# Contiguous first loads, and scaling by a diagonal product, in the first eight passes of a block-causal attention and expert-layer kernel

## The chip, the core and the metric

The kernel runs on one core of a Trainium2 chip. A core has five engines with instruction queues of their own: TensorE (PE in the profile; its weight loads are PEld), VectorE (DVE), ScalarE (ACT), GpSimd (POOL) and SyncE (SP), which here issues the transfers. Each queue is worked in order; engines wait for one another through semaphores. Matrix products read SBUF and write PSUM. The metric is the device time of one execution in microseconds, lower is better.

## The reference

Attention over 8 batches and 8 heads, sequence 576, head size 64, with a mask in blocks of 64: a query block sees the key blocks up to its own. Its output, with the heads side by side, goes through a layer that expands 512 to 2048, applies the square of the ReLU, and contracts again.

```python
scores = scale * np.matmul(q, k.transpose(0, 1, 3, 2))
mask = block_i >= block_j
scores = np.where(mask, scores, -1000000000.0)
scores = scores - np.max(scores, axis=-1, keepdims=True)
attn = np.exp(scores)
attn = attn / (np.sum(attn, axis=-1, keepdims=True) + 1e-09)
return np.matmul(attn, v).astype(np.float32)
...
h = x @ w_in
r = np.maximum(h, 0.0)
g = r * r
return (g @ w_out).astype(np.float32)
```

The expert layer's weights come in as 64-bit floats; the kernel makes a high and a low 16-bit part of each.

## The kernel before

**Passes.** Heads are worked in pairs: a pass holds one batch and one pair, with the two heads in the two halves of the 128 partitions. Of the first two batches, the eight passes 0 to 7 (`G_X`, the short passes) take only the query blocks 0, 1 and 2, that is 64, 128 and 192 keys. This gives the first 192 tokens of both batches, 384 in all, which make the first chunk of the expert layer. The query blocks 3 to 8 of these batches follow in passes 8 to 15 and later batches in whole passes; all those run interleaved with products of the expert layer.

**A short pass.** `softmax` does the scores of the three query blocks into one PSUM tile (L450, fp32 products, keys of 64 partitions by head, with the query padded by zeros in the other half), their negated maxima (L488 and L503, DVE), the exponentials with their sums into the tile `p32` (L506, ACT), the sums' reciprocals `rs` (L514 on POOL, L515 on DVE), and then copies each query block's row out of `p32`, scaled by its reciprocal, into `x_rows`: the block of 192 keys on ACT (L521, `XR_ACT` = 1), the two others on DVE (L523). `x_rows` has five slots (`SLOTS`). `turn` transposes its four 128 x 128 blocks on PE against the identity (L560), and copies the result to `x_turned` (L562, ACT in these passes). `values` multiplies by the values (L593) and copies the output to `x` (L600, ACT). Columns that no key fills were set to zero once (L136, L137).

**First loads.** `load_first` brings two passes at a time (four calls), in five transfers: the queries of each head half (L346, two, 96 KB each), the keys (L347, 192 KB), and the values of each of the two passes (L350, 128 KB each). The tile holds, per partition, pass by pass the padded queries of head 0, those of head 1, and the keys. POOL zeroes the padding (L345). The contiguous runs are 768 bytes for queries and keys and 512 for values. Between the calls SP issues expert weights (`load_w1`, L268): `AHEAD` = (0, 1, 1, 1) blocks after the four calls, and the rest of the 16 behind them. Of each block POOL takes low bits (L231) and DVE a maximum (L281); `BS` lists for the first seven blocks the pass behind whose last scaled row (`t["mark"]`) DVE may do so. From the maxima come power-of-two scales per group of four blocks (`pow2_of_max`, L187 to L196, and L290), and from these the 16-bit parts (`weight_parts`, L322 to L327).

**Then.** When the four pairs of a batch are done, `normalize` forms the power-of-two scale of each token from the squares (L639, L651, L656, L668 to L670). With both batches normalized and the first weight parts there, `first_moe` runs (products L734 and L759). `spin` puts filler products on PE at a few places (L213).

**Order.** The program order is not the order of the queues: a scheduler with a simulated timeline (`TLS`) sets each engine's order when the kernel is built. `behind` adds an edge of order without a wait.

The buffers of the short passes (`p_rows`, `p_turned`) are used again by the later passes' rows, `y_rows` and `p_blocks`; `clear_y` and `clear` set their empty columns to zero on POOL.

Of the kernel before, what the change touches and what calls it, by code (L numbers as in the profile page):

```python
# [8 lines left out]
F32 = mybir.dt.float32  # L9
# [5 lines left out]
AF = mybir.ActivationFunctionType  # L15
ALU = mybir.AluOpType
# [3 lines left out]
P = 128  # L20
D = 64
# [45 lines left out]
XR_ACT = 1  # L67
# [6 lines left out]
T3 = 192  # L74
# [8 lines left out]
SLOTS = 5  # L83
# [17 lines left out]
def attention_moe_kernel(ctx: ExitStack, tc: tile.TileContext, qkt, qk, vm, vt, w_in, w_out, out):  # L101
    nc = tc.nc
# [25 lines left out]
    rows32 = p_rows.bitcast(F32)  # L128
# [3 lines left out]
    x_rows = rows32.rearrange("p (s j k) -> p s j k", s=SLOTS, k=2 * P)  # L132
# [3 lines left out]
    nc.vector.memset(x_rows[:, :, 0, D:P], 0.0)  # L136
    nc.vector.memset(x_rows[:, :, 2, 3 * D :], 0.0)  # L137
# [194 lines left out]
    def load_first(b, hp):  # L332

        n = NHP // 2 * b + hp // 2
        if n < 2:
            t = p2.tile([P, 2, 3, T3], F32, tag="kT", name=f"first{n}")
        elif n == 2:
            t = p1.tile([P, 2, 3, T3], F32, tag="xt1", name=f"first{n}")
        else:
            t = p2.tile([P, 2, 3, T3], F32, tag="qk32", name=f"first{n}", bufs=3)  # L340
        v = vraw[n] if n < 2 else p2.tile([P, 2, 5, D], F32, tag="v16", name=f"firstv{n}")
        hps = slice(hp, hp + 2)
        for h in range(2):
            hs, zs = slice(D * h, D * h + D), slice(D - D * h, P - D * h)
            nc.gpsimd.memset(t[zs, :, h], 0.0)  # L345
            nc.sync.dma_start(t[hs, :, h], qkt[b, hps, hs, 0, :T3].rearrange("c p s -> p c s"))  # L346
        nc.sync.dma_start(t[:, :, 2], qkt[b, hps, :, 1, :T3].rearrange("c p s -> p c s"))  # L347
        for c in range(2):
            o = v[:, c, 0:4].rearrange("p (h n) d -> p h n d", h=2)
            nc.sync.dma_start(o, vm[b, hp + c, :, :, 0:2, :])  # L350
            passes[NHP * b + hp + c].update(
                qz=[t[:, c, h] for h in range(2)], kf=t[:, c, 2], chunks=2, v32=o, es=D**-0.5
            )
# [116 lines left out]
    def softmax(t, group, complete):  # L470
# [6 lines left out]
        p32 = p2.tile([P, 1024], F32, tag="p32", name=f"p32_{gu}")  # L477
# [26 lines left out]
        for i, (j, off) in enumerate(group):  # L504
            w = D * (j + 1)
            nc.scalar.activation(  # L506
                p32[:, off : off + w],
                ps[:, off : off + w],
                AF.Exp,
                bias=nmx[:, i : i + 1],  # L510
                scale=es if t["native"] else -1.0,
                accum_out=sm[:, i : i + 1],
            )
        nc.gpsimd.tensor_scalar(sm, sm, 1e-9, 2.0**-A_P, op0=ALU.add, op1=ALU.mult)  # L514
        nc.vector.reciprocal(rs, sm)  # L515
        if t["whole"]:
            for i, (j, off) in enumerate(group):
                w = D * (j + 1)
                o = (y_rows[:, j - 3] if t["first"] else x_rows[:, t["i"] % SLOTS, j])[:, 0:w]
                if t["first"] or i < XR_ACT:  # L520
                    nc.scalar.activation(o, p32[:, off : off + w], AF.Copy, scale=rs[:, i : i + 1])  # L521
                else:
                    t["mark"] = nc.vector.tensor_scalar(  # L523
                        o, p32[:, off : off + w], rs[:, i : i + 1], None, op0=ALU.mult
                    )
            turn(t, group)
            return
# [12 lines left out]
    def turn(t, group):  # L540
# [11 lines left out]
        else:  # L552
            blocks = [x_rows[:, s, j, P * c : P * c + P] for j, c in ((0, 0), (1, 0), (2, 0), (2, 1))]
            todo = [(blocks, x_turned[:, s])]
        pool, tag = (ps_m, "mm") if t["i"] < PT_MM else (ps_x, "x")
        for blocks, o in todo:
            m = len(blocks)
            pt = pool.tile([P, 4, P], F32, tag=tag, name=f"pt_{n_turned}")
            for i, blk in enumerate(blocks):
                nc.tensor.transpose(pt[:, i], blk, ident)  # L560
# [391 lines left out]
```

## Time and profile before

| what | us |
|---|---|
| median of 3 runs | 1059.64 |
| lowest, highest | 1056.55, 1062.74 |
| the profiled execution | 1060.85 |
| its span, first to last instruction | 1058.6 |
| ACT busy in the span | 657.3 |
| DVE busy in the span | 711.6 |
| POOL busy in the span | 75.8 |

The page's slices of the whole span, each 26.5 us, show where the engines are full (tenths of busy time, 9 is 90% or more; PEclk is the granted clock of TensorE in tenths; DMA is the mean busy share of the 16 transfer engines):

```profile
PE   7899999999999999999999999999999999999998
...
DVE  5998787777787898688379579759677626132230
ACT  6697885794796699289278579449658515041230
...
PEclk8899999999999999999999999999999999999999
DMA  8786168686986788478456758557917520000000
```

The eight short passes lie in the first slice and the beginning of the second. Times of the trace are given from the start of the span. A bracket at the end of a timeline row is the idle time of that engine before the row's first instruction, and what ended it.

### The profile page before, as it was taken

The numbers are of one execution on the slowest core, as the hardware profiler recorded it, in microseconds if no ns is written. First come the engines' busy times: TensorE is split into PE (matmuls) and PEld (weight loads), VectorE is DVE, ScalarE is ACT, GpSimd is POOL, SyncE is SP. The second block draws the span as 40 slices with busy tenths as digits, with TensorE's granted clock in tenths as the row PEclk, the third lists the DMA queues.
The fourth block names the chain that finished last, engine by engine and source line by source line (L and its number), as shares of the span: only waits on it lengthen the run. The fifth ranks groups of instructions, "written<-read, shape, count | busy, mean of one in ns | idle before, by whom it ended". The sixth has DMA issues, their size and how long they took to land.

```text
span 1058.6 us, 19069 instructions
## 1 busy us (share of the span) xinstructions
PE 1014.5 (96%) x6899; PEld 542.6 (51%) x6899; DVE 711.6 (67%) x1972; ACT 657.3 (62%) x1668; POOL 75.8 (7%) x183
## 2 busy tenths in 40 slices
PE   7899999999999999999999999999999999999998
PEld 5445444454554554455455455455455555455553
DVE  5998787777787898688379579759677626132230
ACT  6697885794796699289278579449658515041230
POOL 4213130000000000000001001000000000000000
PEclk8899999999999999999999999999999999999999
DMA  8786168686986788478456758557917520000000
GB/s 271 268 286 240 49 203 201 112 163 141 177 170 140 150 155 158 96 142 184 94 119 123 160 118 166 118 113 140 170 32 121 96 58 1 20 11 11 20 1 30
DMA packets 303902, 133.11 MB, mean 126 GB/s; under 512 B 275648, under 2 KB 288960, under 8 KB 303808
## 3 DMA queue, kind: packets, MB, share of 16 engines
q1 hardware_dynamic: 303808, 131.90, 56.5%
q8 instruction: 54, 0.88, 0.3%
q14 instruction: 40, 0.33, 0.1%
HBM read 55.31 MB, written 9.44 MB: 61 GB/s over the span
## 4 chain that ended last, share of the span: by engine, by line
PE 38%; issue 28%; ACT 8%; DVE 8%; DMA 5%; POOL 2%; SPq 0%; POOLq 0%; ACTq 0%; DVEq 0%
PE po L759 21%; PE ph L734 14%; ACT p L506 2%; ACT p_rows L532 2%; PE ps L461 2%; DVE ps L492 2%; PE px L593 2%; DMA p_turned<-p_rows 2%; DMA kT<-k 1%; DMA qT<-qs 1%; POOL sm L514 1%; DVE p_rows L533 1%; ACT r L742 1%; ACT r L740 1%; DVE g L744 1%
## 5 line engine op out<-in xcount | busy, mean ns | idle before, releaser
L734 PE MATMUL ph<-xt,w1h 128*128 128x384 f16 x1536 | 378.0, 327 | 4.4 <-ACT r L740 4.2
L759 PE MATMUL po<-w2h,g 128*128 128x512 f16 x1152 | 352.4, 380 | 3.6 <-ACT r L740 2.0
L759 PEld LDWEIGHTS <-g 128*128 128x128 f16 x1728 | 165.9, 98 | 202.4 <-issue 11.5
L734 PE MATMUL ph<-xt,w1l 128*128 128x384 f16 x768 | 251.0, 327 | 0.0
L759 PE MATMUL po<-w2l,g 128*128 128x512 f16 x576 | 218.8, 380 | 0.7 <-DVE w2l L327 0.7
L506 ACT ACTIVATE p<-ps,nmx 128x192 f32<-128x192 f32 (+8 forms) x288 | 149.0, 532 | 109.7 <-DVE nmx L492 86.2
L734 PEld LDWEIGHTS <-w1h 128*128 128x128 f16 x1536 | 143.3, 98 | 110.0 <-issue 21.0
L740 ACT ACTIVATE r<-ph 128x384 f32<-128x384 f32 x192 | 94.1, 493 | 120.2 <-PE ph L734 119.1
L533 DVE SCALAR_TENSOR_TENSOR p_rows<-p,rs,p_rows 128x384 f16<-128x384 f32 (+4 forms) x264 | 128.9, 525 | 22.1 <-ACT p_rows L532 18.4
L532 ACT ACTIVATE p_rows<-p,rs 128x384 f16<-128x384 f32 (+4 forms) x264 | 125.3, 550 | 14.3 <-DVE rs L515 9.7
L492 DVE CUSTOM_DVE_ANT_0 ps<-ps,zero,es 128x128 f32<-128x128 f32 (+8 forms) x216 | 117.5, 550 | 23.8 <-PE ps L461 22.3
L766 DVE TENSOR_SCALAR ob<-po,uv 128x512 f32<-128x512 f32 x36 | 29.1, 808 | 142.7 <-PE po L759 142.7
L744 DVE TENSOR_TENSOR g<-r,g 128x384 f16<-128x384 f32 x192 | 105.5, 553 | 2.9
L743 DVE CAST g<-r 128x384 f16<-128x384 f32 x192 | 67.0, 353 | 59.0 <-ACT r L742 58.9
L742 ACT ACTIVATE r<-r 128x384 f32<-128x384 f32 x192 | 100.8, 530 | 2.7
L734 PEld LDWEIGHTS <-w1l 128*128 128x128 f16 x768 | 75.3, 98 | 49.4 <-issue 0.5
L514 POOL TENSOR_SCALAR sm<-sm 128x2 f32<-128x2 f32 (+2 forms) x104 | 37.6, 362 | 697.9 <-ACT p L506 591.8
L461 PE MATMUL ps<-kT,qT 128*64 128x64 f16 (+6 forms) x960 | 80.8, 290 | 6.9 <-ACT p L506 3.0
L593 PE MATMUL px<-p_turned,v 128*64 128x64 f16 (+5 forms) x1168 | 76.5, 270 | 7.1 <-DMA p_turned<-p_rows 5.6
L593 PEld LDWEIGHTS <-v 128*64 128x64 f16 x1128 | 53.5, 110 | 32.8 <-issue 21.6
L461 PEld LDWEIGHTS <-qT 128*64 128x64 f16 x960 | 45.2, 110 | 41.5 <-issue 27.7
L506 ACT ACTIVATION_READ_ACCUMULATOR p<-ps,nmx 128x1 f32 x288 | 60.6, 211 | 0.0
(139 smaller groups left out, 859.0 us busy)
## 6 DMA issues: line engine op xcount, KB each, us to landing
qk<-in_qk SPq DMA_DIRECT2D x24, 576.0 KB, 4.9
wa<-in_w_out SPq DMA_DIRECT2D x16, 512.0 KB, 5.7
out<-ob SPq DMA_DIRECT2D x32, 256.0 KB, 2.3
vraw<-in_vm SPq DMA_DIRECT2D x30, 256.0 KB, 3.7
w1raw<-in_w_in SPq DMA_DIRECT2D x8, 512.0 KB, 6.7
wb<-in_w_out SPq DMA_DIRECT2D x8, 512.0 KB, 5.1
kf<-in_qkt SPq DMA_DIRECT2D x8, 288.0 KB, 4.1
w2h<-in_w_in SPq DMA_DIRECT2D x4, 512.0 KB, 9.7
```

The costliest lines, as they stand in the source:

```text
L461: nc.tensor.matmul(ps[hs, o].rearrange("p (n d) -> p n d", d=D), t["qT"][:, j, hs], t["kT"][:, z, c0:c1, hs], start=(z == 0), stop=(z == 1),)
L492: nc.vector.tensor_tensor_reduce(ps[:, off : off + w], ps[:, off : off + w], zero.to_broadcast([P, w]), es, 3e38, op0=ALU.add, op1=ALU.min ...
L506: nc.scalar.activation(p32[:, off : off + w], ps[:, off : off + w], AF.Exp, bias=nmx[:, i : i + 1], scale=es if t["native"] else -1.0, acc ...
L532: nc.scalar.activation(hi, p, AF.Copy, scale=rs[:, i : i + 1])
L533: nc.vector.scalar_tensor_tensor(lo, p, rs[:, i : i + 1], hi, op0=ALU.mult, op1=ALU.subtract)
L593: nc.tensor.matmul(px[hs, D * a :].rearrange("p (j d) -> p j d", d=D), lhs, rhs, start=(c == 0 and pi == 0), stop=(c == NCH[g] - 1 and (pi ...
L734: nc.tensor.matmul(ph[:, :CH], w[:, f, P * cc : P * cc + P], xt[:, z, cc, :], start=(i == 0), stop=(i == 11))
L740: nc.scalar.activation(r, ph[:, :CH], AF.Relu, scale=c)
L742: nc.scalar.activation(r, r, AF.Square)
L743: nc.vector.tensor_copy(g[:, 0], r)
L744: nc.vector.tensor_tensor(g[:, 1], r, g[:, 0], op=ALU.subtract)
L759: nc.tensor.matmul(po, gs[f][:, z, P * t : P * t + P], w[:, f, :], start=(i == 0), stop=(i == 3 * NF - 1))
```

## The change

Three things change, all for the short passes.

1. The host lays out two more inputs, `qk1` and `v1`. A pair of passes is loaded by three transfers: for each head half, queries and keys together, in runs of 3072 bytes (keys and queries lie in the other order for the second half, so that the key rows of both halves meet in the middle third of the tile); and the values of both passes, in runs of 1024 bytes. The tile's layout is now queries of head 0, keys, queries of head 1, each for both passes.
2. The exponentials are written straight into the slot of `x_rows`, unscaled, instead of into `p32`. The copies that scaled them go. DVE instead makes three diagonal matrices, the identity times the reciprocals, in one operation, in the same slot (`x_diag`).
3. The four blocks of a pass are turned by fp32 products with those matrices as the moving operand, which turn and scale at once, instead of by transposes against the identity. There are four slots instead of five, of seven blocks each. The mark for the weight maxima is now the diagonal operation.

```diff
-SLOTS = 5
+SLOTS = 4
...
-    x_rows = rows32.rearrange("p (s j k) -> p s j k", s=SLOTS, k=2 * P)
+    x_slots = rows32[:, : SLOTS * 7 * P].rearrange("p (s b k) -> p s b k", s=SLOTS, k=P)
+    x_rows, x_diag = x_slots[:, :, 0:4], x_slots[:, :, 4:7]
...
-    nc.vector.memset(x_rows[:, :, 0, D:P], 0.0)
-    nc.vector.memset(x_rows[:, :, 2, 3 * D :], 0.0)
+    for b in (1, 3):
+        nc.vector.memset(x_rows[:, :, b, D:P], 0.0)
...
+        shape = [P, 3, 2, T3]
...
-            nc.gpsimd.memset(t[zs, :, h], 0.0)
-            nc.sync.dma_start(t[hs, :, h], qkt[b, hps, hs, 0, :T3].rearrange("c p s -> p c s"))
-        nc.sync.dma_start(t[:, :, 2], qkt[b, hps, :, 1, :T3].rearrange("c p s -> p c s"))
+            nc.gpsimd.memset(t[zs, 2 * h], 0.0)
+            nc.sync.dma_start(t[hs, h : h + 2], qk1[n, hs])
+        nc.sync.dma_start(v[:, :, 0:4], v1[n])
         for c in range(2):
-            o = v[:, c, 0:4].rearrange("p (h n) d -> p h n d", h=2)
-            nc.sync.dma_start(o, vm[b, hp + c, :, :, 0:2, :])
...
-        p32 = p2.tile([P, 1024], F32, tag="p32", name=f"p32_{gu}")
+        short = t["whole"] and not t["first"]
+        if short:
+            p32 = x_rows[:, t["i"] % SLOTS].rearrange("p b k -> p (b k)")
+            at = {2: 0, 1: 2 * P, 0: 3 * P}
...
+        if short:
+            t["mark"] = nc.vector.tensor_tensor(
+                x_diag[:, t["i"] % SLOTS],
+                ident[:, None, :].to_broadcast([P, n, P]),
+                rs[:, :, None].to_broadcast([P, n, P]),
+                op=ALU.mult,
+            )
+            turn(t, group)
+            return
...
-                if t["first"] or i < XR_ACT:
-                    nc.scalar.activation(o, p32[:, off : off + w], AF.Copy, scale=rs[:, i : i + 1])
-                else:
-                    t["mark"] = nc.vector.tensor_scalar(
-                        o, p32[:, off : off + w], rs[:, i : i + 1], None, op0=ALU.mult
-                    )
...
-            blocks = [x_rows[:, s, j, P * c : P * c + P] for j, c in ((0, 0), (1, 0), (2, 0), (2, 1))]
+            blocks = [(x_rows[:, s, b], x_diag[:, s, j]) for b, j in ((3, 2), (2, 1), (0, 0), (1, 0))]
...
-                nc.tensor.transpose(pt[:, i], blk, ident)
+                if t["first"]:
+                    nc.tensor.transpose(pt[:, i], blk, ident)
+                else:
+                    nc.tensor.matmul(pt[:, i], blk[0], blk[1], start=True, stop=True)
...
+    qk1 = qkt[..., :T3].reshape(2, 2, 2, P, 2, T3).transpose(0, 1, 3, 4, 2, 5).reshape(4, P, 2, 2, T3)
+    qk1 = np.concatenate([qk1[:, :D], qk1[:, D:, ::-1]], axis=1)
+    v1 = vm[:2, :, :, :, :2].reshape(2, 2, 2, P, 4, D).transpose(0, 1, 3, 2, 4, 5).reshape(4, P, 2, 4, D)
```

More of the change, by code (lines that the diff above doesn't have):

```diff
@@ L334, in load_first @@
         n = NHP // 2 * b + hp // 2
+        shape = [P, 3, 2, T3]
         if n < 2:
-            t = p2.tile([P, 2, 3, T3], F32, tag="kT", name=f"first{n}")
+            t = p2.tile(shape, F32, tag="kT", name=f"first{n}")
         elif n == 2:
-            t = p1.tile([P, 2, 3, T3], F32, tag="xt1", name=f"first{n}")
+            t = p1.tile(shape, F32, tag="xt1", name=f"first{n}")
         else:
-            t = p2.tile([P, 2, 3, T3], F32, tag="qk32", name=f"first{n}", bufs=3)
+            t = p2.tile(shape, F32, tag="qk32", name=f"first{n}", bufs=3)
         v = vraw[n] if n < 2 else p2.tile([P, 2, 5, D], F32, tag="v16", name=f"firstv{n}")
-        hps = slice(hp, hp + 2)
         for h in range(2):
             hs, zs = slice(D * h, D * h + D), slice(D - D * h, P - D * h)
-            nc.gpsimd.memset(t[zs, :, h], 0.0)
-            nc.sync.dma_start(t[hs, :, h], qkt[b, hps, hs, 0, :T3].rearrange("c p s -> p c s"))
-        nc.sync.dma_start(t[:, :, 2], qkt[b, hps, :, 1, :T3].rearrange("c p s -> p c s"))
+            nc.gpsimd.memset(t[zs, 2 * h], 0.0)
+            nc.sync.dma_start(t[hs, h : h + 2], qk1[n, hs])
+        nc.sync.dma_start(v[:, :, 0:4], v1[n])
         for c in range(2):
-            o = v[:, c, 0:4].rearrange("p (h n) d -> p h n d", h=2)
-            nc.sync.dma_start(o, vm[b, hp + c, :, :, 0:2, :])
             passes[NHP * b + hp + c].update(
-                qz=[t[:, c, h] for h in range(2)], kf=t[:, c, 2], chunks=2, v32=o, es=D**-0.5
+                qz=[t[:, 2 * h, c] for h in range(2)],
+                kf=t[:, 1, c],
+                chunks=2,
+                v32=v[:, c, 0:4].rearrange("p (h n) d -> p h n d", h=2),
+                es=D**-0.5,
             )
@@ L506, in softmax @@
             nc.scalar.activation(
-                p32[:, off : off + w],
+                p32[:, at[j] : at[j] + w],
                 ps[:, off : off + w],
@@ L518, in softmax @@
                 w = D * (j + 1)
-                o = (y_rows[:, j - 3] if t["first"] else x_rows[:, t["i"] % SLOTS, j])[:, 0:w]
-                if t["first"] or i < XR_ACT:
-                    nc.scalar.activation(o, p32[:, off : off + w], AF.Copy, scale=rs[:, i : i + 1])
-                else:
-                    t["mark"] = nc.vector.tensor_scalar(
-                        o, p32[:, off : off + w], rs[:, i : i + 1], None, op0=ALU.mult
-                    )
+                o = y_rows[:, j - 3, 0:w]
+                nc.scalar.activation(o, p32[:, off : off + w], AF.Copy, scale=rs[:, i : i + 1])
             turn(t, group)
@@ L943 @@
     arrays, args = {}, []
-    for name, a in (("qkt", qkt), ("qk", qk), ("vm", vm), ("vt", vt), ("w_in", w1), ("w_out", w2)):
+    for name, a in (("qk1", qk1), ("v1", v1), ("qkt", qkt), ("qk", qk), ("vm", vm), ("vt", vt), ("w_in", w1), ("w_out", w2)):
         arrays[f"in_{name}"] = a
```

7 lines of the change are left out of this document (5 added, 2 removed).

## The prediction, made before the changed kernel was run

> **What bounds the kernel now.** First the page, for the engine that sets the length.
>
> ```profile
> span 1058.6 us, 19069 instructions
> ...
> PE 1014.5 (96%) x6899; PEld 542.6 (51%) x6899; DVE 711.6 (67%) x1972; ACT 657.3 (62%) x1668; POOL 75.8 (7%) x183
> ```
>
> TensorE (PE) is busy for 96% of the span. Busy time by stretch (length, then PE, PEld, DVE, ACT, POOL with their instruction counts, clock, DMA share, GB/s) shows where the missing 44 us lie:
>
> ```profile
> core 0: us, PE busy (x) PEld busy (x) DVE busy (x) ACT busy (x) POOL busy (x), PEclk, DMA share, GB/s
> 0.00:50.00 50.00, 39.75 (x304) 26.03 (x305) 37.46 (x118) 31.78 (x98) 19.94 (x52) 0.86 0.84 275
> 50.00:100.00 50.00, 46.87 (x283) 25.53 (x280) 45.51 (x115) 42.72 (x99) 12.13 (x23) 0.97 0.83 282
> ```
>
> Ten of the 44 idle us are in the first 50, at a mean granted clock of 0.86. The change touches only the eight short passes there and what loads them, so I treat the kernel as a front that ends when the first product of the expert layer starts, and a rest that begins when the front ends. A microsecond saved in the front is worth at most one at the end. The timeline of the front shows what releases what:
>
> ```profile
> 5.28 1.67 PE L450 MATMUL ps<-first 128*64 128x192 f32 x24 [0.72 <-DMA first<-in_qkt]
> 8.86 0.97 PE L450 MATMUL ps<-first 128*64 128x192 f32 x12 [1.91 <-ACT p L506]
> 11.49 1.54 PE L560 MATMUL pt<-ident,p_rows 128*128 128x128 f32 x6
> 13.86 1.53 PE L450 MATMUL ps<-first 128*64 128x192 f32 x11 [0.83 <-DMA first<-in_qkt]
> 17.88 0.33 ACT L600 ACTIVATE x<-px 128x192 f32<-128x192 f32 x1 [1.16 <-PE px L593]
> 25.34 0.66 PE L593 MATMUL px<-p_turned,firstv 128*64 128x192 f32 x8 [1.16 <-ACT p_turned L562]
> 27.15 0.36 DVE L656 TENSOR_SCALAR hb<-nq 128x192 int32<-128x192 int32 x1 [0.53 <-PE nq L213]
> 47.54 0.33 PE L734 MATMUL ph<-xt,w1h 128*128 128x384 f16 x1
> ```
>
> Read as three stages. Up to 17.9 us, PE and the loads lead: PE waits for the first loads (5.28) and the third (13.86), and ScalarE (ACT) waits for PE (17.88). From there to about 27 ACT leads: PE waits for ACT's copy at 25.34. From 27.15 to 47.54 VectorE (DVE) leads. The stretches agree:
>
> ```profile
> 10.30:13.00 2.70, 2.70 (x19) 2.16 (x18) 1.68 (x10) 2.08 (x8) 0.50 (x1) 0.57 1.01 278
> 13.00:17.80 4.80, 3.97 (x33) 3.40 (x34) 2.50 (x11) 2.33 (x9) 2.02 (x6) 0.53 1.01 279
> 17.80:25.00 7.20, 6.01 (x68) 4.49 (x64) 5.36 (x20) 7.12 (x31) 3.07 (x9) 1.00 1.02 399
> 30.00:40.00 10.00, 6.18 (x50) 4.09 (x49) 10.00 (x25) 2.56 (x6) 6.15 (x10) 0.90 1.04 338
> ```
>
> PE runs at 0.57 and 0.53 of its clock from 10.3 to 17.8; ACT is busy 7.12 of 7.20 us after that; DVE 10.00 of 10.00 from 30 to 40.
>
> **The loads.** SyncE (SP) issues five transfers per pair of heads:
>
> ```profile
> 0.75 1.44 SPq L346 DMA_DIRECT2D first<-in_qkt  x2
> 2.24 0.60 SPq L347 DMA_DIRECT2D first<-in_qkt  x1
> 2.88 1.23 SPq L350 DMA_DIRECT2D vraw<-in_vm  x2
> 15.14 5.07 SPq L268 DMA_DIRECT2D w1raw<-in_w_in  x6
> DMA packets 2196, 2.16 MB, mean 270 GB/s; under 512 B 171, under 2 KB 1940, under 8 KB 2196
> DMA packets 1921, 4.57 MB, mean 381 GB/s; under 512 B 173, under 2 KB 918, under 8 KB 1918
> ```
>
> (The first packet row is 8 to 16 us, the second 16 to 28.) An issue takes about 0.62 us. Three instead of five saves 1.2 us per pair, 5 us over four pairs, so the six weight transfers that start at 15.14 could be issued from about 10. The packets say the same of the engines: 984 B on average give 270 GB/s in the first stretch, 2379 B give 381 in the second. The four pairs are 4 x 640 KB, 2.62 MB: 9.7 us at the one rate, 6.9 at the other. The last weights should land 2.8 to 5 us earlier; I use 3. What that is worth on the path is less:
>
> *First scores.* They wait for the third transfer, issued by 2.84. Queries and keys now are in two, issued by 2.19, so they start 0.6 earlier. The row allows at most 0.72, the idle time, and nothing if the two larger transfers take that much longer. **-0.6**; ends -0.7 and 0. The next step, 8.86, waits for ACT's exponentials of the same pass and moves with it.
>
> *Fifth pass.* The wait of 0.83 at 13.86 goes, because the third pair is issued about 2.4 us earlier. Late next is PE itself, whose work before that ends at 13.03 (11.49 + 1.54). **-0.8**; ends -0.83 and 0.
>
> *Queues passed.* The weight transfers overtake nothing that the passes need, since each pair still stands ahead of its weights. On POOL the low-bit operation of the first weight block waits for its load with the sum of pass 2 behind it; earlier weights only shorten that. POOL's memsets are as many as before.
>
> **The scaling of the rows.** It leaves ACT (L521) and DVE (L523), and one product of the identity with the reciprocals comes to DVE.
>
> ```profile
> L521 ACT ACTIVATE p_rows<-p,rs 128x192 f32<-128x192 f32 x8 | 3.9, 485 | 0.5 <-DVE rs L515 0.5
> L523 DVE TENSOR_SCALAR p_rows<-p,rs 128x128 f32<-128x128 f32 x8 | 3.0, 372 | 0.2
> L523 DVE TENSOR_SCALAR p_rows<-p,rs 128x64 f32<-128x64 f32 x8 | 2.0, 246 | 0.0
> L668 DVE TENSOR_TENSOR x<-x,hb 128x768 f32<-128x768 f32 x1 | 1.0, 959 | 0.0
> 43.40 0.67 DVE L327 TENSOR_TENSOR w1l<-w1raw,w1h 128x512 f16<-128x512 f32 x1
> 14.61 0.45 DVE L523 TENSOR_SCALAR p_rows<-p,rs 128x128 f32<-128x128 f32 x2
> ```
>
> DVE: 768 columns take 959 ns and 512 take 670, 1.13 ns a column, so 384 take 0.53 us. The two operations that go take 0.45 together when nothing disturbs them and 0.62 by their means. Between +0.08 and -0.09 per pass, of which two passes lie in or beside the DVE stage: nothing.
>
> ACT: 8 x 0.485 = 3.9 us of work go. Only what lies in the ACT stage counts, three of them between 17.9 and 25.3, at most 1.46 us. PE is next: it is busy 6.01 of those 7.20 us before it gets more work, so the gain cannot all be kept. **-0.6**, below half; ends -1.46 and 0.
>
> **The turning.** Four transposes per pass become four fp32 products. What one costs is read from the scores, which are fp32 products now:
>
> ```profile
> L560 PE MATMUL pt<-ident,p_rows 128*128 128x128 f32 x32 | 6.4, 324 | 0.3
> L450 PE MATMUL ps<-first 128*64 128x128 f32 x32 | 4.3, 310 | 0.0
> 29.60 0.66 PE L560 MATMUL pt<-ident,p_rows 128*128 128x128 f32 x4
> L560 PE MATMUL pt<-ident,p_rows 128*128 128x128 f32 x8 | 1.5, 291 | 0.1
> L560 PE MATMUL pt<-ident,p_rows 128*128 128x128 f32 x8 | 2.2, 435 | 0.0
> ```
>
> (The last two rows are the transposes alone, at full clock from 20 to 24 us and at the low clock from 10.8 to 17.) Eight passes with four blocks make 32 transposes, one instruction each. Eight passes with two heads make 16 score calls of 128 columns, and these are 32 instructions of much the same length: an fp32 product is two instructions. So a pass gets eight for four. Four take 0.66 at 29.60, of which the first is 0.29 and each further one 0.12; eight take 0.29 + 7 x 0.12 = 1.13, **+0.48 per pass** at full clock. At the low clock six took 1.54 (11.49), 0.435 and five of 0.22; four more add **0.88**. All eight passes are between 8 x 0.48 = 3.8 and 8 x 0.88 = 7.0 us of PE work. On the path: three of them (passes 0 to 2) stand ahead of the values that ACT waits for at 17.88, at the low clock, 2.6 us. PE's idle time between 8.0 and 10.3 covers a part:
>
> ```profile
> 8.00:10.30 2.30, 1.30 (x14) 1.06 (x14) 1.07 (x6) 2.15 (x13) 0.39 (x2) 1.00 0.89 239
> ```
>
> That is 1.0 us, and because the scaled rows are not awaited the first products can start in it. **+1.7**; ends +2.6 and +0.4 (three at full clock, less the cover). In the ACT stage their cost is already why I kept only 0.6.
>
> **The clock.** It is 1.00 to 10.3 us, low to 17.8 and 1.00 again. Taken as a half until it is whole again, the mean of 0.53 over 4.8 us puts the return near 17.5, some 3.5 us after PE's last wait ended (13.86). If the wait goes and PE has more to do, the same return comes before the end of the stage: one such stretch, 3.5 us of work at half clock, done in half the time. **-1.7**; ends -3.0 (6.67 us of busy PE time at about 0.55 would be 3.7 at full clock) and 0.
>
> [...]
>
> **The sum.** -0.6 - 0.8 - 0.6 + 1.7 - 1.7 = **-2.0 us**. The span goes from 1058.6 to 1056.6. The profiled execution took 1060.85, 2.25 above its span and 1.2 above the median of the three runs, 1059.64, which I move by the same 2.0: **1057.6 us**. For the DVE stage to begin earlier, its weights must be there:
>
> ```profile
> 38.47 0.65 POOL L231 TENSOR_SCALAR w2l<-w2l 128x512 int32<-128x512 uint16 x1 [0.95 <-DMA w2l<-in_w_in]
> 40.28 0.66 DVE L281 TENSOR_REDUCE stw<-w2l 128x1 f32<-128x512 f32 x1
> ```
>
> The last block lands at 38.47 and its maximum begins at 40.28, so without faster loads only about 1.2 us (after POOL's operation) could be kept; 3 us of earlier landing cover the 2.0.
>
> **Rivals.**
>
> *The clock stays up.* Terms: -0.6 - 0.8, products +0.4, ACT -1.46, clock -3.0: -5.5, so 1054.1. For it: the dense work from 9 us on. Against: PE's idle time up to 10.3 remains, as it comes from ACT. Chance 0.18, half beyond 0.5%.
>
> *The products become the bound, slower.* All eight at the low clock: 8 x 0.88 = 7.0, less 0.6, 0.8 and 1.46: +4.1, so 1063.7. It decides if the clock is still below 1.00 past 18 us; a little more and it passes 0.5%. For it: PE is full from 10.3 to 13.0. Against: the clock returned with less work. Chance 0.14, half beyond 0.5%.
>
> *The long runs bring no speed.* Each query and key transfer now fills 64 partitions, and how fast that is alone no row shows. Then the weights hold DVE at 40.28 and 1.2 us is the most: 1058.4. Chance 0.15.
>
> *The planner orders DVE anew.* The weight maxima are queued by a simulated timeline. Group 0's last maximum was followed by its scale only at 40.04:
>
> ```profile
> 25.11 0.14 DVE L287 TENSOR_REDUCE st<-stw 128x1 f32<-128x4 f32 x1
> 40.04 0.13 DVE L290 TENSOR_SCALAR wsc<-wm 128x1 int32<-128x1 int32 x1
> ```
>
> Some 15 us for small operations queued behind large ones. If they move up by 4, the weight parts and the first products do: -6, 1053.6. Chance 0.12. The same freedom can cost as much; that is in the slower chance.
>
> My forecast has 0.41. Half a per cent, 5.3 us, is about what a measurement of this kernel can tell from no change. Faster by more: half of the first rival, most of the last, a little of the forecast, 0.24. Slower by more: 0.11. Within: 0.65. The range goes from 1051 (a little past the fast rivals) to 1063.5 (the slow one nearly).
>
> **What would show it.** Right: the first scores start near 4.7, the fifth pass's without a DMA wait, a turning of eight instructions lasts about 1.1 us at full clock, the clock is back before 16, DVE fills up near 25, and the first expert product starts near 45.5. Wrong: PE without a gap from 9 to 25 at the low clock, DVE waiting for the last weights, or an expert layer whose start moves and whose end does not.

## The result, and the profile after

| | before | after |
|---|---|---|
| median, us (lowest to highest) | 1059.62 (1056.55 to 1062.74, 6 runs) | 1066.35 (1063.93 to 1067.71, 6 runs) |
| ratio to before, 95% interval | 1 | 1.0061 (1.0039 to 1.0083) |
| profiled execution | 1060.85 | 1067.44 |
| its span | 1058.6 | 1065.7 |

The changed kernel is 0.6% slower. 1057.6 us was forecast, with a range to 1063.5, so the prediction was wrong by 8.8 us and in the sign.

The page's slices of the whole span, after (tenths of busy time in 26.6 us each):

```profile
PE   7899899999989989999999999999999999999998
...
DVE  4999587777887889578379569759677716132230
ACT  4797785786796599289288569549657615042230
...
PEclk9999899999999999999999999999999999999999
DMA  9768157788798597466746659557817530000000
```

In the first slice the granted clock is higher than before (9 for 8), and the transfers are too. But PE has an 8 in the fifth slice (106 to 133 us) where the clock has an 8 too, and more 8s up to the fifteenth. That is long behind the eight short passes.

**The front, after.** From the timeline: PE at the short passes' start, then POOL and DVE.

```profile
4.51 0.63 PE L213 MATMUL ps<-ones_bf 128*128 128x512 bf16 x1
5.07 1.64 PE L452 MATMUL ps<-first 128*64 128x192 f32 x24
8.63 1.88 PE L452 MATMUL ps<-first 128*64 128x192 f32 x24 [1.92 <-ACT p_rows L514]
13.72 1.16 PE L575 MATMUL pt<-p_rows 128*128 128x128 f32 x8 [3.21 <-DVE p_rows L525]
15.51 2.05 PE L575 MATMUL pt<-p_rows 128*128 128x128 f32 x8 [0.63 <-DVE p_rows L525]
```

```profile
11.95 0.64 POOL L231 TENSOR_SCALAR w1raw<-w1raw 128x512 int32<-128x512 uint16 x1 [4.23 <-DMA w1raw<-in_w_in]
12.67 0.47 POOL L522 TENSOR_SCALAR sm<-sm 128x3 f32<-128x3 f32 x2
```

```profile
12.90 0.18 DVE L523 RECIPROCAL rs<-sm 128x3 f32<-128x3 f32 x1 [5.11 <-POOL sm L522]
13.11 0.56 DVE L525 TENSOR_TENSOR p_rows<-ident,rs 128x384 f32<-128x384 f32 x1
```

Read it backwards. The first products (13.72) wait for the diagonal (13.11), this for the reciprocal (12.90), this for the sums on POOL (12.67). POOL had the sums' inputs by 9.6 us (ACT's last exponential of pass 1) but waited 4.23 us for the first weight block: its low-bit operation now stood *ahead* of the sums of passes 0 and 1. Before, both sums stood ahead of it. The earlier loads moved it: with the loads alone (c1 below) it stands ahead of both sums too, with the products alone (d1) it does not.

**Where the 6.7 us appear.** To compare two traces stage by stage, I added up PE's necessary products in order (scores, values, expert layer, each counted by its columns), and took the time by which each kernel had done the same amount. The table gives that time less the one of before, in us; the second row is the end of the front.

| time in before | after | a1 | b1 | d1 | e1 | i1 | j1 | k1 |
|---|---|---|---|---|---|---|---|---|
| 20.0 | +3.1 | +3.0 | -1.6 | -0.7 | -2.1 | -1.7 | -0.2 | +1.4 |
| 44.4 | -2.2 | -1.7 | -1.1 | +0.1 | -2.6 | -2.7 | +0.3 | -2.3 |
| 118.5 | -0.6 | +1.6 | +2.4 | -0.1 | -2.0 | +0.1 | -1.3 | -4.2 |
| 134.7 | +5.4 | +1.6 | +6.8 | +1.3 | -2.0 | +0.1 | -1.3 | -4.2 |
| 165.6 | +8.3 | +2.3 | +7.9 | +2.4 | -1.8 | +1.2 | -0.5 | -2.7 |
| 356.5 | +3.4 | -2.0 | +3.9 | -1.1 | -5.2 | -3.0 | -3.5 | -6.1 |
| 401.8 | +6.7 | +2.1 | +7.8 | +7.1 | +2.7 | +1.1 | -3.0 | -0.5 |
| 940.5 | +6.7 | +1.3 | +7.5 | +5.9 | +0.2 | -0.5 | -4.1 | -1.6 |

(The columns behind "after" are experiments below; each is one profiled execution.) After is 3.1 us late at 20 us, which is POOL's wait, but 2.2 us *ahead* when the front ends, and 0.6 ahead at 118 us. Then it loses 9 us up to 166 us, and again 3 at 357 to 402. The loss is in work that the change does not touch.

**The stretch at 118 us.** PE by the timeline, first before, then after:

```profile
118.05 0.55 PE L560 MATMUL pt<-ident,p_rows 128*128 128x128 f32 x3 [0.79 <-DVE p_turned L562]
118.52 1.73 PE L450 MATMUL ps<-kf,qz 128*64 128x512 f32 x8
120.18 0.17 PE L194 MATMUL pm_w<-dg_w,ones_bf 1*128 1x1 bf16 x1
120.28 0.77 PE L560 MATMUL pt<-ident,p_rows 128*128 128x128 f32 x5
121.30 1.19 PE L450 MATMUL ps<-kf,qz 128*64 128x320 f32 x8 [0.25 <-ACT p L506]
```

```profile
117.87 3.21 PE L452 MATMUL ps<-kf,qz 128*64 128x512 f32 x8 [1.03 <-ACT p L514]
121.01 0.70 PE L573 MATMUL pt<-ident,p_rows 128*128 128x128 f32 x3
121.65 0.17 PE L194 MATMUL pm_w<-dg_w,ones_bf 1*128 1x1 bf16 x1
122.28 0.76 PE L573 MATMUL pt<-ident,p_rows 128*128 128x128 f32 x5 [0.46 <-ACT p_turned L577]
124.78 2.19 PE L452 MATMUL ps<-kf,qz 128*64 128x320 f32 x8 [1.73 <-ACT p L514]
```

The same products, but after has the eight scores ahead of the three transposes in PE's queue. Two things are seen: the waits are 1.03 and 1.73 us where they were 0.79 and 0.25, and the same eight scores take 3.21 us for 1.73, the next 2.19 for 1.19. The second is the clock. Four windows of 3.4 us, before and then after (length; PE busy and instructions; granted clock; DMA share; GB/s):

```profile
114.60:118.00 3.40, 1.76 (x12) 1.00 0.16 49
118.00:121.40 3.40, 3.10 (x19) 1.00 0.00 0
121.40:124.80 3.40, 3.40 (x29) 1.00 0.12 34
124.80:128.20 3.40, 2.86 (x18) 1.00 0.42 116
```

```profile
114.60:118.00 3.40, 1.47 (x12) 1.00 0.02 6
118.00:121.40 3.40, 3.40 (x10) 0.50 0.00 0
121.40:124.80 3.40, 1.21 (x11) 1.00 0.00 0
124.80:128.20 3.40, 3.40 (x14) 0.50 0.00 0
```

In after, a window in which PE is busy for 1.47 or 1.21 us is followed by one at exactly half clock. At a clock of 0.50 a window of 3.4 us full of work does 1.7 us of work less (an estimate from these two). The trace of after has five such windows behind 45 us (from 70.2, 118.0, 124.8, 169.2 and 387.6 us), that of before two (75.5 and 324.7): three more, up to 5.1 us. This holds for the two profiled executions. The six executions of after have mean clocks of 0.989 to 0.994, and the profiled one is the lowest of them, so the average has less of it; and g1 below, with one such window behind 45 us, and k4, with none, have spans of 1062.3 and 1060.2 us against 1058.6. The half clock is a part of the loss, not all of it.

### The profile page after: what moved, and what is told of

It is laid out like the page before. It is cut to its first block, busy times and chain, and to the rows that moved or that the text cites. A ratio compares the mean times of both kernels' runs of the same rounds, so it can differ in the third digit from the quotient of the medians.

```text
span 1065.7 us, 19102 instructions
## 1 busy us (share of the span) xinstructions
PE 1019.7 (96%) x6931; PEld 543.9 (51%) x6931; DVE 709.5 (67%) x1964; ACT 657.1 (62%) x1660; POOL 78.6 (7%) x183
## 4 chain that ended last, share of the span: by engine, by line
PE 52%; issue 22%; DVE 12%; DMA 7%; ACT 6%; POOL 1%; SPq 0%; POOLq 0%; ACTq 0%; DVEq 0%
PE po L774 22%; PE ph L749 19%; PE px L608 4%; PE ps L452 3%; PE ps L463 3%; DMA kT<-k 2%; DMA p_turned<-p_rows 2%; DVE ps L500 2%; ACT p L514 2%; ACT p_rows L544 1%; DVE stw L281 1%; DVE nmx L496 1%; DVE p_rows L545 1%; DMA qT<-qs 1%; POOL sm L522 1%
## 5 line engine op out<-in xcount | busy, mean ns | idle before, releaser
L774 PEld LDWEIGHTS <-g 128*128 128x128 f16 x1728 | 165.6, 98 | 201.6 <-issue 9.2
L514 ACT ACTIVATE p<-ps,nmx 128x576 f32<-128x576 f32 (+8 forms) x264 | 140.1, 543 | 97.5 <-DVE nmx L500 83.6
L463 PE MATMUL ps<-kT,qT 128*64 128x64 f16 (+5 forms) x960 | 81.4, 290 | 8.3 <-DMA qT<-qs 4.3
L514 ACT ACTIVATION_READ_ACCUMULATOR p<-ps,nmx 128x1 f32 x264 | 54.8, 207 | 0.0
```

The lines of the kernel that those rows point to most:

```text
L463: nc.tensor.matmul(ps[hs, o].rearrange("p (n d) -> p n d", d=D), t["qT"][:, j, hs], t["kT"][:, z, c0:c1, hs], start=(z == 0), stop=(z == 1),)
L514: nc.scalar.activation(p32[:, at[j] : at[j] + w], ps[:, off : off + w], AF.Exp, bias=nmx[:, i : i + 1], scale=es if t["native"] else -1.0, ...
L774: nc.tensor.matmul(po, gs[f][:, z, P * t : P * t + P], w[:, f, :], start=(i == 0), stop=(i == 3 * NF - 1))
```

## The experiments

Of each kernel the ratio to the kernel before is given, measured on the same chip in the same job, with its 95% interval. "Old order" is the order that the planner gave the kernel before.

### Is it the order or the front? a1, b1, c1, d1

Theory O: the planner's new order of the later work costs the time. Theory F: the front's own work does. The 9819 instructions traced behind the short passes are the same in both kernels; their queue order is not (2096 of 6476 on PE stand elsewhere, 773 of 1623 on DVE, 512 of 1226 on ACT). a1 holds the changed kernel to the old order by edges without waits, b1 the kernel before to the new order:

```diff
+    body = len(traced())
     todo.append(first_moe(0, firsts))
...
     while todo or waiting:
         fill(1)
+    made = traced()[body:]
+    for at in ORDER.values():
+        for a, b in zip(at, at[1:]):
+            tc.add_manual_dep(
+                made[b],
+                made[a].name,
+                mybir.DependencyInfo(mybir.DependencyClass.NoSync, mybir.DependencyReason.DATA),
+                reason="order given",
+            )
```

c1 has only the new loads (the hunks of `load_first` and of the host), d1 only the diagonal products (the other hunks).

> The changed kernel, with everything traced behind the eight short passes and their normalization (9819 instructions) held in the queue order that it has in the kernel before; the front is the changed kernel's own. Theory O (the loss is the order that the planner gave to the later work): 1056 to 1060 us, ratio to before 0.997 to 1.001. Theory F (the loss comes from the front itself, its late sums on POOL and its longer products): 1064 to 1068, as the changed kernel.

> The kernel before, with the same 9819 instructions held in the queue order that they have in the changed kernel; loads, scaling and turning are the old ones. Theory O: 1064 to 1069 us, since the order alone carries the loss (about 6 us or more). Theory F: 1058 to 1061, no change.

> Only the contiguous loads, on the kernel before; the planner is free. The later queues differ from those of before in 280 of 6476 places on PE, where those of the changed kernel differ in 2096. Theory O: within 3 us of before, either side. Theory F, if earlier weights put POOL's low-bit operation ahead of the sums: 3 to 7 us slower.

> Only the unscaled rows and the diagonal products, with the old loads; the planner is free, and its later PE queue differs in 221 of 6476 places. Theory O: within 3 us of before. Theory F, if the products are the loss: 3 to 7 us slower.

| run | median, us | ratio (95%) |
|---|---|---|
| a1 changed, old order | 1062.30 | 1.0041 (1.0023 to 1.0060) |
| b1 before, new order | 1071.29 | 1.0102 (1.0079 to 1.0126) |
| c1 loads alone | 1062.45 | 1.0020 (1.0003 to 1.0037) |
| d1 diagonal alone | 1065.96 | 1.0058 (1.0041 to 1.0076) |

b1 settles that an order can cost more than the whole loss: nothing of the change is in it, and it is 1.0% slower. It shows the same two stalls as after at the same place:

```profile
120.94 1.73 PE L473 MATMUL ps<-kf,qz 128*64 128x512 f32 x8 [1.03 <-ACT p L529]
...
126.20 2.19 PE L473 MATMUL ps<-kf,qz 128*64 128x320 f32 x8 [1.72 <-ACT p L529]
```

The waits of 1.03 and 1.72 us come with the order, scores ahead of transposes. The half clock does not come with it one to one: here the first eight scores ran at the full clock (1.73), the others at half (2.19). a1 went down by about 4 us but its interval overlaps that of after, and it did not reach before. d1, whose front is not slower, lost as much as the whole change. Its later queue differs from the old order in 221 places only, and its time lies in the range of Theory F (3 to 7 us slower). c1 lost 2 us by the ratio and 3 by the medians, at the border of its two ranges. a1 lies between its two ranges, and b1 above both of its own.

### POOL's wait, and more about the order: e1, f1, g1, h1

Theory P: what a1 kept is POOL's wait in the front. e1 and f1 put the low-bit operations behind the sums again:

```diff
+    AFTER_SUM = {0: 1, 1: 3, 2: 4, 3: 5, 5: 6, 7: 7}
...
+        for f, i in AFTER_SUM.items():
+            behind(lows[f], sums[i])
         clear_y()
```

e1 is held to the old order besides, f1 is not. g1 is d1 in the old order. h1 is the changed kernel in the old order as far as what stood at 168 us, and in its own from there on.

> The changed kernel, with the low-bit operations of the first weight blocks put on POOL's queue behind the sums of the short passes, as they stood before, and with all work behind the short passes held in the old order (as in a1, which took 1062.3 us). Theory P (what a1 kept of the loss is the 4.2 us wait of POOL for the first weight block in front of two sums): the first diagonal stands near 9.5 us instead of 13.1, the lag of 3 us at 28 us goes, and the time is that of before or a little below, 1057 to 1060 us. Rival R (the diagonal products or the earlier transfers cost it in themselves): 1062 us again, whatever POOL does.

> The changed kernel with the same edges on POOL's queue and nothing else: the rest is ordered anew by the planner, and comes out nearer to the old order than the changed kernel's (250 of 6476 PE instructions stand elsewhere than before, against 2096). Theory P with the order theory: 1057 to 1062 us, most of the 6.7 us gone by one edge per weight block. If the order were of no account and the front's work the cause: 1064 to 1067. If any other order is as bad as the changed one: about 1066 as well, with the front's lag gone.

> The diagonal products alone, on the old transfers, with all work behind the short passes held in the old order (free, they took 1065.96 us though their front was 0.2 to 1.1 us ahead of before). Order theory: 1058 to 1060 us, no slower than before. Theory F (the products themselves cost it): 1064 to 1067 us as when free.

> The changed kernel with the old order in the work behind the short passes as far as what stood at 168 us before, and its own order from there on. 408 PE instructions change their place against the changed kernel. If the 5 to 6 us are lost in the stretch 115 to 168 us, as the two traces with the new order show: 1060 to 1063 us, like a1. If the order is bad throughout: 1065 to 1067.

| run | median, us | ratio (95%) |
|---|---|---|
| e1 changed, sums first, old order | 1061.08 | 1.0027 (1.0016 to 1.0038) |
| f1 changed, sums first | 1063.36 | 1.0035 (1.0018 to 1.0052) |
| g1 diagonal alone, old order | 1064.14 | 1.0053 (1.0034 to 1.0073) |
| h1 changed, old order to 168 us | 1067.03 | 1.0087 (1.0067 to 1.0107) |

None came within the range of Theory P or of the order theory. g1 came within that of Theory F (1064 to 1067 us): it was as slow in the old order as d1 in its own, so Theory O in the form "the old order is good" falls, and the products are suspect in themselves. h1 is inconclusive: it lost its 7 us just at the seam between the two orders (PE idle for 5.1 us from 162.8 us). e1 is the telling one. Its sums are no longer held up, and its front is what the prediction had asked for:

```profile
8.51 0.20 POOL L548 TENSOR_SCALAR sm<-sm 128x3 f32<-128x3 f32 x1 [0.99 <-ACT p_rows L540]
9.47 0.19 POOL L548 TENSOR_SCALAR sm<-sm 128x3 f32<-128x3 f32 x1 [0.77 <-ACT p_rows L540]
11.43 0.68 POOL L257 TENSOR_SCALAR w1raw<-w1raw 128x512 int32<-128x512 uint16 x1 [1.76 <-DMA w1raw<-in_w_in]
```

By the table it is 2.6 us ahead at the front's end, 2.0 at 118 us, 5.2 at 357. Then all of it goes in 45 us. PE there, first a row of the timeline of e1 and the same one of before, then windows of 3.4 us of e1 and of before:

```profile
382.77 0.27 PE L634 MATMUL px<-p_turned,v 128*64 128x192 f16 x2 [2.66 <-DMA p_turned<-p_rows]
```

```profile
384.79 0.27 PE L593 MATMUL px<-p_turned,v 128*64 128x192 f16 x2 [0.91 <-DMA p_turned<-p_rows]
```

```profile
380.30:383.70 3.40, 0.93 (x7) 1.00 1.30 168
383.70:387.10 3.40, 3.40 (x21) 0.50 1.01 207
387.10:390.50 3.40, 3.40 (x28) 1.00 0.13 24
```

```profile
380.30:383.70 3.40, 3.40 (x37) 1.00 1.07 239
383.70:387.10 3.40, 2.49 (x21) 1.00 1.65 237
387.10:390.50 3.40, 3.40 (x38) 1.00 0.73 160
```

PE arrives at the values of pass 22 earlier than the transposing transfers of its rows, which moreover take longer; it waits 2.66 us, where before waited 0.91. The window with 0.93 us of work is followed by half clock. The same happens again at 397.4 to 404.2 us (1.35 us of work in the first window, a clock of 0.50 in the second). Two such windows are 3.4 of the 7.9 us that e1 loses by the table between 357 and 402 us; its two waits before them are 2.66 us and, at 400.58, 2.05.

**What the products have to do with it.** This loss is no matter of one draw. By the same count of PE's work, every kernel with the products, in whatever order, loses 3.0 to 8.0 us against before between 357 and 402 us. Of those without them, b1 (the new order) loses 3.8, and c1, i2, j1, j2 and l2 (the kernels not met so far are described below) lose between -0.2 and 1.5. The traces show a likely reason. The rows of pass 22 are turned by four transfers, and the values wait for the second. From its issue to the start of the values, the transfer queues carried (name and kind: packets, MB, time), first in e1 (376.84 to 382.77 us), then in before (379.99 to 384.79):

```profile
q1 hardware_dynamic: 2453, 1.11, 105.6%
q8 instruction: 1, 0.02, 1.2%
```

```profile
q1 hardware_dynamic: 2458, 1.11, 107.1%
```

The one packet on queue q8 is 16 KB of kind "instruction". Each whole trace has 54 of them; PE has 13,798 products and weight loads in before, 64 more in after, so a packet comes once in some 255 of PE's instructions, and I take them for PE's program (an estimate from the counts). In the eleven kernels with the products whose order is the old one or near it there (a1, d1 to g1, i1, k1 to k4, l1), such a packet starts between the landings (the ends) of the first and the second transfer, and the second lands 2.70 to 3.00 us after the first. In before, c1, i2, j1, j2 and l2 it starts after the second has landed, and that lands 1.47 or 1.48 us after the first. If these packets are PE's program, 64 more instructions ahead make them come that much earlier in the later work. No run moved the packet on purpose, so this is read from the traces, not shown by an experiment.

### The half clock itself: i1, i2

Theory C: the windows at half clock, set off by such stalls, are a cost beside the stalls. i1 is e1, and i2 the kernel before in its own order, with 21 products of ones put into PE's queue at three places where e1 stalled for about 2 us; the products write a PSUM region that the next real product resets or nobody reads.

```diff
+        if t["i"] == 24 and group[0][0] == 4:
+            keep(ps[:, 0:512], 5, "before next")
...
+        if t["i"] == 22 and g == 0:
+            keep(full[:, w:], 8, "before next")
...
+        if b == 2 and g == 0:
+            keep(full[:, w:], 8, "behind last")
```

> As e1_sums_first_old_order (1061.08 us), with 21 matmuls of ones that nobody reads put into TensorE's queue at three places where e1 stalled for about 2 us: 8 of 320 columns behind the norms of the third batch (before the product at 318.7), 8 of 320 before the value products of pass 22 (382.8), 5 of 512 before the first scores of pass 24 (400.6), about 1.1 us of work at each place, inside the stall. Theory C (a stall that leaves TensorE busy for under 0.43 of a 3.41 us window is followed by 3.41 us at half clock, which costs 1.7 us more than the stall): the half-clock windows at 319, 384 and 401 us are gone, and the time falls by 1.7 to 4 us, to 1057 to 1059.5. Rival S (the stalls alone are the cost, the clock follows and costs nothing of its own): 1061 as before, or up to 3.2 us longer where a place is no stall.

> The kernel before, its order held, with the same 21 matmuls at the same three places, where its profile shows stalls of 1.96, 0.91 and 0 us. Theory C: at most one half-clock window (the one at 324.7 us) is saved and the others' dummies cost up to 1.2 us where there is no stall: 1057 to 1060 us, less gain than in i1. Rival S: 1059 to 1061.

| run | median, us | ratio (95%) |
|---|---|---|
| i1 e1 with fillers | 1058.98 | 0.9991 (0.9976 to 1.0006) |
| i2 before with fillers | 1058.04 | 0.9989 (0.9973 to 1.0005) |

i1 against e1: from 1.0027 to 0.9991, and the intervals do not touch. Its PE at pass 22:

```profile
382.39 1.26 PE L238 MATMUL px<-ones_bf 128*128 128x320 bf16 x8
385.16 0.27 PE L655 MATMUL px<-p_turned,v 128*64 128x192 f16 x2 [1.51 <-DMA p_turned<-p_rows]
```

```profile
380.30:383.70 3.40, 3.35 (x28) 1.00 1.53 226
383.70:387.10 3.40, 1.94 (x13) 1.00 0.89 198
```

The stall of 1.26 + 1.51 = 2.77 us is as long as in e1, but 1.26 us of it is filled, the window has 1.94 us of work, and the clock stays at 1.00. i1 is in the range of Theory C and below that of Rival S: 21 idle products took 0.36% off by the ratios and 2.1 us off the median, and the mean clock of twelve executions each rose from 0.9955 to 0.9971. Theory C holds, Rival S falls. In the kernel before, with shorter stalls there, the same ones took at most a little: the interval reaches 1.

### Other orders drawn: j1, j2, k1 to k4

The planner's order follows from its timeline, and one dummy product (`SPIN`, L213) more or less at the very start gives another: 196 and 199 PE instructions elsewhere for ten and eight dummies in the kernel before. j1 and j2 are the kernel before, k1 and k2 the changed kernel, k3 and k4 the changed kernel with the sums first. k3 has the later order of k1, and k4 that of k2; only the edges on POOL differ.

```diff
-SPIN = (9, {5: 4, 6: 4, 7: 4}, 5, 8)
+SPIN = (10, {5: 4, 6: 4, 7: 4}, 5, 8)
```

(8 for 10 in j2, k1 and k3.)

> The kernel before with ten dummy matmuls instead of nine ahead of the first scores, and nothing else: no time is taken from or given to any stage by it (the front waits for loads there), but the planner sets 196 PE, 103 DVE and 65 ACT instructions of the later work elsewhere. If the time is a matter of how stalls fall in the later work, and the order of before was a favourable one: 1061 to 1066 us. If orders are worth the same on the average and the change's own work costs: 1058 to 1060.

> The same with eight dummy matmuls: another order (199 PE, 98 DVE, 70 ACT instructions elsewhere). Same expectations: 1061 to 1066 if any displacement of the later work loses against before, 1058 to 1060 if not. A time below before's would show that the change could as well have been drawn a good order.

> The changed kernel with eight dummy matmuls instead of nine ahead of the first scores. The later work comes out near the order of before (150 of 6476 PE instructions elsewhere, against 2096 with nine); on POOL the low-bit operation of the first weight block stands ahead of the sum of pass 1 and that of the second ahead of the sum of pass 3. If the changed kernel's order was an unlucky draw and POOL's wait costs 2 us: 1059 to 1063 us. If the change costs 6 us by itself: 1065 to 1067.

> The changed kernel with ten dummy matmuls: 330 of 6476 PE instructions elsewhere than before, and POOL's queue as in the changed kernel (the first low-bit operation ahead of the sums of passes 0 and 1). Same expectations: 1059 to 1063 for a drawn order with POOL's wait, 1065 to 1067 if the change costs it by itself.

> As k1, with the low-bit operations behind the sums on POOL's queue; the later order is the same as in k1. If POOL's wait costs: 1 to 3 us less than k1, and 1056 to 1060 us. If the later work gives the front's time back in any case: the same as k1.

> As k2, with the low-bit operations behind the sums; the later order is the same as in k2. POOL's wait costs: 1 to 3 us less than k2, and 1056 to 1060 us. Otherwise the same as k2. With f1 (1063.4 us) the mean of k3 and k4 tells what the change is worth: 1057 to 1058 if the predicted 2 us are there, 1059 to 1060 if they are lost, 1062 and more if the products cost time.

| dummies | before | changed | changed, sums first |
|---|---|---|---|
| 8 | j2 1.0015 (0.9998 to 1.0032) | k1 0.9997 (0.9980 to 1.0014) | k3 1.0003 (0.9985 to 1.0020) |
| 9 | 1 | after 1.0061 (1.0039 to 1.0083) | f1 1.0035 (1.0018 to 1.0052) |
| 10 | j1 0.9980 (0.9965 to 0.9996) | k2 1.0048 (1.0031 to 1.0066) | k4 1.0057 (1.0037 to 1.0076) |

j1 (1057.30 us) came below both of its ranges, and k2 (1064.91) between its two. Three readings. First, the kernel before was no favourable draw, since j1 is below it. Secondly, the changed kernel can be drawn as fast as before: with one dummy less it takes 1059.25 us. In that draw 150 PE instructions stand elsewhere than in the old order, against 2096 in after. But that is one draw of three. The means of the three rows are 0.9998, 1.0035 and 1.0032, and f1, k3 and k4 take 1063.0 us on the average, where 1062 and more was to mean that the products cost time. Three draws with such a spread settle no size, but they do not clear the change. Thirdly, k4 and k2 are alike within their intervals, and k3 and k1 too. By the count of PE's work k2 is 2.7 us behind k4 at 20 us and 1.2 at the end of the front; the medians show none of it at the end. The three pairs that differ in POOL's queue alone (a1 and e1, k1 and k3, k2 and k4) differ by -0.0014, 0.0006 and 0.0009, on the average by nothing, give or take about 1.5 us (an estimate from their intervals). POOL's wait, plain as it is in the front, is not what made the kernel slower: Theory P falls too.

### The best of both: l1, l2

k1 and j1, each held to its own order, with the 21 fillers.

> k1 (the changed kernel with eight dummy matmuls, 1059.25 us) with its order held and the 21 matmuls of i1 at the same three places, where k1's profile shows stalls of 1.96, 3.53 and 1.51 us and half-clock windows at 319.0 and 383.9 us. Theory C: 1.7 to 3.4 us less than k1 where the grid falls as in k1's profile, on the average 1 to 3: 1056.5 to 1058.5 us, a version that is as fast as any so far. Rival S: 1059 to 1061.

> j1 (the kernel before with ten dummy matmuls, 1057.3 us) with its order held and the same 21 matmuls; its profile shows stalls of 1.97, 1.47 and 1.39 us there and no half-clock window behind them. Theory C: at most 1 us less on the average, 1056 to 1058 us. If the change has kept its 2 us of the front, l1 lies 1 to 2 us below this; if not, they are alike or this is the lower.

| run | median, us | ratio (95%) |
|---|---|---|
| l1 changed, 8 dummies, fillers | 1057.76 | 0.9980 (0.9965 to 0.9995) |
| l2 before, 10 dummies, fillers | 1054.81 | 0.9956 (0.9942 to 0.9970) |

l2, which has nothing of the change, is the fastest of all: 0.44% below before, and below the 1056 to 1058 us expected. l1 does not lie 1 to 2 us below it, as it was to if the change kept its 2 us, but 2.9 above by the medians; the two intervals just overlap. In l1 the fillers do not quite reach: its profile still has a wait of 2.39 us at pass 22 and one half-clock window behind it, from 378.9 us. Both compared kernels are beaten by an order and 21 idle products, by more than the change was forecast to bring.

## Why the prediction was wrong

Its terms can be read in e1, whose front is the one that was forecast, and in after.

- **First scores, -0.6:** too large. They start at 5.07 in after and 4.98 in e1, for 5.28, a gain of 0.2 to 0.3. No wait for the queries and keys stands before them; PE's own nine dummies end only then (the row at 4.51). With eight dummies (k1) they start at 4.84.
- **Fifth pass, -0.8:** right in kind. It does not wait for a transfer in after or e1; in e1 its scores start at 12.79 for 13.86, after 0.48 us of waiting for POOL.
- **Turning, +0.48 per pass at full clock:** right. Eight products take 1.16 us (13.72) for the 1.13 worked out, and 2.05 (15.51) at the low clock for 0.435 + 7 x 0.22 = 1.98. The diagonal takes 0.56 us (13.11) for 0.53. The term on the path is a little off by its own working: 2.6 less 1.0 is +1.6, not +1.7.
- **The clock, -1.7:** right in kind for after, and exceeded in e1. Windows of 10 us, e1 (columns as above):

```profile
0.00:10.00 10.00, 6.83 (x53) 1.00 0.76 212
10.00:20.00 10.00, 9.36 (x108) 1.00 1.05 310
20.00:30.00 10.00, 8.66 (x86) 1.00 1.02 404
```

  Before has 0.66 and after 0.83 in the second of these; e1 has 1.00. But the products do not secure it: k3 and k4, whose sums are not held up either, have 0.83 there, k2 has 0.66, and b1, with transposes, has 1.00. Low windows come with products (k2) and with transposes (before).
- **The sum of the front, -2.0:** the first expert product starts at 45.30 in e1 for 47.54, -2.24. In after it starts early too, at 45.79, though POOL's wait was not foreseen. That the sum fits is in part luck, as the first scores and the clock show. And neither half brings the gain alone: by the count of PE's work c1 and d1 stand within 0.1 us of before at 44.4 us.
- **"Queues passed" failed in the front.** The step said that of POOL "earlier weights only shorten that" wait. It took POOL's queue as fixed. The planner put the first low-bit operation ahead of two sums; the 4.23 us row is the price: 3.1 us at 20 us, repaid at 44, and by the pairs above nothing at the end.
- **The step that failed for the time** is the last one of the sum, "which I move by the same 2.0": it carried the front's gain to the end unchanged, and put the effect on the later work at nothing because the change "touches only the eight short passes". Of the pairs drawn with the same dummies one shows such a gain (j2 1.0015, k1 0.9997); the two others show 0.6 and 0.7% the other way. e1 took 2.6 us to the end of the front and lost it at 375 to 405 us; k4 ends where k2 does, with 2.7 us between them in the front. The change reaches the later work in two ways: the planner set 2096 of 6476 PE instructions elsewhere, and the products put 64 more instructions ahead of it. What came out at the end was set by PE's stalls in the next 400 us: 9 us lost from 118 to 166 us in after, 3.0 to 8.0 us from 357 to 402 us in every kernel with the products (and 3.8 in b1).
- **The rival "the planner orders DVE anew" named one of the two ways, mis-sized.** It was seen only for 15 us of small operations on DVE, with a price of -6 and a chance of 0.12, and its cost side was one sentence. The order of a third of PE's later instructions changed; as a draw it moves this kernel between 0.9980 and 1.0102 (j1, b1). That alone is a range of 1057 to 1070 us.
- Of the signs named at the end, "an expert layer whose start moves and whose end does not" is what came.

So after lost its time from 118 to 166 us and from 357 to 402 us, with half-clock windows behind stalls in both stretches, and b1 shows both losses with the new order alone. But the old order would not have kept the gain: in it, or near it, the kernels with the products lose in the second stretch at pass 22, and a1 is still 0.41% slower than before. Three things stay open. How the loss divides between the order and the products is not settled, as the intervals of a1 and after overlap. That the instruction packet is what delays the transfers of pass 22 is read from the traces and not tested; after, b1 and h1, whose order differs there, do not bear on it. And which of the moved instructions cost most was shown for one place (118 us) and not summed up.

## What to carry to other kernels

When a planner with a simulated timeline orders the queues, a change at the start is a change of every queue behind it: compare the two orders before pricing the change, draw two or three neighbouring orders (one dummy more or less), and take their spread as the resolution of the comparison. A microsecond gained ahead of a long stretch in which one engine is nearly full is worth something only if the stretch's other engines and transfers can follow (e1's 2.6 us at the end of the front were lost around PE's waits of 2.66 and 2.05 us for transfers); look for the first place where the full engine waits for them. Instructions added at the start may also move later packets of kind "instruction" (read here at pass 22, where the second transfer landed 2.70 to 3.00 us after the first with such a packet between and 1.47 or 1.48 without; not tested): where a wait for a transfer has grown for no reason in the order, look for such packets in that stretch. Where TensorE waits for some 2 us and half clock follows, idle products inside the wait can cost less than that half clock: 21 of them took 2.1 us off e1's median.

## What the runs showed of the hardware

**In these traces the half clock lasted 3.41 us or a multiple of it, and 34 of the 35 windows in which PE was busy for less than 0.43 were followed by it.** In the clock records of all twenty traces every stretch at half clock lasts 3.41 us or a multiple (6.83 us from 10.66 and from 37.97 us in before, 3.41 from 75.52 and 324.69), but for the last, which the end of the trace cuts off, and within a trace all begin on one grid. Counting for each such window behind 45 us how much of it PE was busy, and whether the next was at half clock (windows themselves at half clock left out; a window or two at the edge between two rows go to either side by how the grid is rounded):

| PE busy in the window | windows | followed by half clock |
|---|---|---|
| under 0.40 | 20 | 20 |
| 0.40 to 0.43 | 15 | 14 |
| 0.43 to 0.54 | 39 | 11 |
| over 0.54 | some 5700 | 0 |

Single windows of the count, by PE's busy time in 3.41 us: 1.64 (from 72.10 us) and 1.45 (321.28) in before, and 1.44 (66.77), 1.00 (165.76) and 1.33 (384.21) in after were followed by a clock of 0.50; 1.57 (421.76) in after was followed by 1.00. PE's single wait in such a window was 1.03 us in after (ending at 117.87) and 2.66 in e1 (ending at 382.77); those windows had 1.47 and 0.93 us of work in 3.40.

**The grid lies otherwise in each of the twenty traces, and a part of the spread goes with the granted clock.** Half clock begins at 75.52 us in before and at 70.19 in after, 1.56 windows apart. Much the same stall is followed by half clock in one trace and not in another: a wait of 1.95 or 1.96 us near 322 us is in before, a1 and g1 and was followed by half clock in before alone. The ten runs of d1, the same instructions each time, go from 1061.22 us at a mean clock of 0.995 to 1070.92 at 0.985; 0.010 of 1066 us is 10.7, and they differ by 9.7. That the place of the grid makes this difference is the author's inference and was not shown. Nor does the clock go with all of the spread: e1's slowest execution (1063.51 us) has 0.997, and one of 1059.94 has 0.994.

**In pass 22, the only place where it was read, transposing transfers with the start of a 16 KB instruction packet between their landings landed further apart.** There the second transfer lands 1.47 or 1.48 us after the first without such a packet between (six kernels) and 2.70 to 3.00 with it (eleven). In i2 and l2 the packet falls between the second and the third instead, and there the third lands 2.86 and 2.90 us after the second, for 1.34 or 1.35 in before, c1, j1 and j2.
